# Query-tile norm moved wholly to GpSimd, weight conversion paced by kind of slot, start-up loads interleaved, half steps reordered

## The chip, the cores and the metric

One core of one Trainium2 chip runs the whole program. The metric is device time in microseconds of one execution. TensorE multiplies (PE in the profile, its weight loads PEld), VectorE (DVE) and ScalarE (ACT) work on elements, GpSimd (POOL) does so too, but only on on-chip memory that is not PSUM, and SyncE (SP) issues the transfers. Each engine runs its own instructions strictly in the order in which the program has them, and waits on semaphores for the others.

## The reference

```python
scale = 1.0 / np.sqrt(np.sqrt(D))                 # D = 64, m = 128 features
def phi(x):                                       # q, k: 4 batches, 8 heads, 576 rows
    h = x @ omega.T - np.sum(x * x, -1, keepdims=True) / 2
    return np.exp(h - h.max(-1, keepdims=True)) / np.sqrt(m)
q_p, k_p = phi(q * scale), phi(k * scale)
kv = einsum('bhsm,bhsd->bhmd', k_p, v);  z = k_p.sum(axis=2)
x = (q_p @ kv) / (q_p @ z + 1e-6)                 # to 2304 tokens x 512
xn = x / sqrt(mean(x*x) + 1e-6) * rms_g           # the norm this change moves
g = xn @ w_gate                                   # 512 -> 1536
y = (g * sigmoid(g) * (xn @ w_val)) @ w_out       # 1536 -> 512
h = y @ w_in                                      # 512 -> 2048
out = (h * cos(h)) @ w_out2                       # 2048 -> 512
```

All inputs are float32. The term -sum(x*x)/2 and the 1/sqrt(m) fall out of the quotient, so the kernel does not compute them.

## The kernel before

The 2304 tokens are 18 tiles of 128; a block is 3 tiles (384 columns), so there are 6 blocks. A float32 product is made of three products of float32r halves (`mm3`): every weight chunk of 128 x 512 is split into a high and a low part on the chip ("conversion", class `Weights`).

**Conversion** of one chunk c is a generator: ScalarE writes W (L138), VectorE does four instructions (L153, L155, L157, L160), GpSimd adds (L164), the load of chunk c + 3 is issued on SP, ScalarE rounds to w (L170), GpSimd subtracts (L172). `wts.tick(n)` advances it by n of these seven steps; the instructions land in the engines' queues where the call stands. `wts.pace(rate)` does the same with a fractional count.

**Attention** runs in slots. A slot projects one tile of keys or queries (`project`, 16 matmuls into two PSUM banks), takes the row maxima on VectorE and eight exponentials on ScalarE (`features`). A key tile is multiplied with its values one slot later (`kv_product`). A query tile t goes on through six later steps (`query_step`): 1 turn the features (eT) and copy them out, 2 sums and quotients (num, den, x), 3 square on ScalarE (sq), 4 `root` and `norm`, 5 turn x (xT) and copy the high part (`put(t, 0)`), 6 the low part on VectorE (`put(t, 1)`), after every third tile with a store to DRAM. The norm before is: VectorE scales and shifts the mean square (L281), GpSimd raises it to the power -1/2 (L282), VectorE multiplies x by it and by the gain (L286).

Slots 0 to 22 hold the 18 key tiles and query tiles 0 to 4 (slots 6, 9, 12, 15, 22); from slot 9 to 17 a period is one query tile and two key tiles. From slot 23 on each slot is a half step of the first feed-forward layer: step n is slots 23 + 2n and 24 + 2n, in each the 12 matmuls of `product` (gv) and, for the step before, 6 of `out1` (y), and query tiles 5 to 17 start at slots 24, 26, 29, 32, 34, 37, 40, 42 and so on, three in eight. ScalarE needs another function table for Silu than for the exponential.

PSUM banks with tag "w" (four, handed out in turn) hold gv, qp or kp (two), xT and, in the half steps, also eT and num. A product that gets a bank waits until whoever reads the bank's last holder is done.

Within a slot the order is that of the code: `slot_before` does steps 6 and 4 of older tiles, `slot_after` begins the new tile and does steps 5, 3, 2, 1 of older ones and the key-value product. `manual_schedule` means that the engines get their instructions in this order.

Of the kernel before, what the change touches and what calls it, by code (L numbers as in the profile page):

```python
# [38 lines left out]
AF = mybir.ActivationFunctionType  # L39
ALU = mybir.AluOpType  # L40
# [13 lines left out]
def attention_then_ffn(ctx: ExitStack, tc: tile.TileContext, qT, kT, v, omT, wc1, rms_g, wc2, out, B, H, S, D):  # L54
    nc = tc.nc
    M = omT.shape[1]
    DM = H * D
# [43 lines left out]
    def f32(ap):  # L101
        return ap.bitcast(F32)
# [3 lines left out]
    quarter = const.tile([P, 1], F32, name="quarter")  # L106
    half_pi = const.tile([P, 1], F32, name="half_pi")
# [6 lines left out]
    class Weights:  # L114
# [26 lines left out]
        def run(self):  # L141

            last = len(self.todo)
            for c in range(3):
                self.load(c)
            yield
            self.exponent(0)
            yield
            for c in range(last + 1):
                if c < last:  # L150
                    w, raw = self.w.pop(c), self.raw.pop(c)
                    f = conv.tile([P, 512], I32, tag="f", name=f"f{c}", bufs=3)
                    nc.vector.tensor_scalar(f, w, 3, None, op0=ALU.logical_shift_left)  # L153
                    yield
                    nc.vector.scalar_tensor_tensor(f, w, SIGN, f, op0=ALU.bitwise_and, op1=ALU.bitwise_or)  # L155
                    yield
                    nc.vector.tensor_scalar(raw[:, :, 1], f, SIGN_AND_EXPONENT, None, op0=ALU.bitwise_and)  # L157
                    yield
                    rest = f32(raw[:, :, 1])
                    nc.vector.scalar_tensor_tensor(rest, raw[:, :, 0].bitcast(U32), 2.0 ** -52, rest,  # L160
                                                   op0=ALU.mult, op1=ALU.mult)
                    self.exponent(c + 1)
                    yield
                    nc.gpsimd.tensor_tensor(f32(f), f32(f), rest, op=ALU.add)  # L164
                    self.f[c] = f32(f)
                    yield
                    self.load(c + 3)
                if c > 0:
                    t = wpool.tile([P, 2, 512], F32R, tag="w", name=f"w{c - 1}")
                    nc.scalar.copy(t[:, 0], self.f[c - 1])  # L170
                    yield
                    nc.gpsimd.tensor_tensor(t[:, 1], self.f.pop(c - 1), f32(t[:, 0]), op=ALU.subtract)  # L172
                    self.out[self.todo[c - 1]] = t
                    self.done = c
                    yield
# [20 lines left out]
    wts = Weights()  # L196


    class Attention:
# [41 lines left out]
        def keep_transposed(self, t, r):  # L241
            ps = self.ps.pop(("eT", t, r))
            eT = self.tile_of("featT", [P, HP, P], F32, f"eT{t}_{r}")
            ps = ps.rearrange("p (h n) -> p h n", h=HP)
            if r or self.tag == "w":
                nc.scalar.copy(eT, ps)
            else:
                nc.vector.tensor_copy(eT, ps)
            self.eT[t, r] = eT
# [26 lines left out]
            ms = self.ms[t] = self.tile_of("ms", [P, 1], F32, f"ms{t}")  # L276
            nc.scalar.activation(sq, self.x[t], AF.Square, accum_out=ms)

        def root(self, t):
            ms = self.ms[t]  # L280
            nc.vector.tensor_scalar(ms, ms, 1.0 / DM, 1e-6, op0=ALU.mult, op1=ALU.add)  # L281
            nc.gpsimd.tensor_tensor(ms, ms, minus_half, op=ALU.pow)  # L282

        def norm(self, t):
            a = self.x[t]
            nc.vector.scalar_tensor_tensor(a, a, self.ms.pop(t), self.gain, op0=ALU.mult, op1=ALU.mult)  # L286

        def load_gain(self):
            self.gain = self.tile_of("gain", [P, DM], F32, "gain")
# [32 lines left out]
    with tc.manual_schedule():  # L322
# [7 lines left out]
        att = Attention(  # L330
            lambda what, shape, dt, name: ap.tile(shape, dt, tag=what, name=name, bufs=depth.get(what, 2)), "q", kv)
# [4 lines left out]
        def load_v(t):  # L336
            if t < NTILE:
                nc.sync.dma_start(vt[t % NV][:, 0:H], v[t])
# [28 lines left out]
        def query_step(t, s):  # L367

            if s == 1:
                for r in range(2):  # L370
                    att.transposed(t, r)
                    att.keep_transposed(t, r)
            elif s == 2:
                for r in range(2):
                    att.sums(t, r)
                    att.quotients(t, r)
            elif s == 3:
                att.square(t)
            elif s == 4:
                att.root(t)  # L380
                att.norm(t)
            elif s == 5:
                att.turn(t)
                att.put(t, 0)
            elif s == 6:
                att.put(t, 1)
                if t % TPB == TPB - 1:
                    store(t // TPB, "x")
# [7 lines left out]
        SLOTS = len(tiles)  # L396
# [3 lines left out]
        begins, then = {}, {}  # L400
        for s, (nm, t) in tiles.items():
            if nm == "k":
                for i in range(len(parts(t))):
                    then.setdefault(s + 1 + i, []).append((1, kv_product, t, i))
            else:
                for i in range(1, 7):
                    then.setdefault(s + i, []).append((-i, query_step, t, i))
        for todo in then.values():
            todo.sort(key=lambda e: e[0])
        AHEAD = 2  # L410
        order = sorted(tiles)

        def slot_before(s):

            at = order.index(s) if s in tiles else -1
            if at >= 0 and at + AHEAD < len(order):
                att.load(*tiles[order[at + AHEAD]])
            for k, f, *args in then.get(s, []):
                if k in (-6, -4):
                    f(*args)  # L420

        def slot_after(s):
            if s in tiles:
                att.project(*tiles[s])
                for r in range(2):
                    att.features(*tiles[s], r)
            for k, f, *args in then.get(s, []):
                if k not in (-6, -4):
                    f(*args)

        nc.sync.dma_start(om, omT)
        att.load(*tiles[0])
        att.load(*tiles[1])
        load_v(0)
        wts.tick(1)
        load_v(1)
        load_v(2)
        att.load_gain()
        for a in vt:
            nc.vector.memset(a[:, H], 1.0)  # L440
        for a in kv:
            nc.vector.memset(a[:, H * (D + 1):], 0.0)
        make_identity(nc, ident)
        nc.gpsimd.memset(quarter, 0.25)
        nc.gpsimd.memset(half_pi, math.pi / 2)
        nc.gpsimd.memset(minus_half, -0.5)
        nc.vector.tensor_scalar(om, om, SCALE, None, op0=ALU.mult)

        UP = 9
        for s in range(SLOTS):  # L450
            slot_before(s)
            slot_after(s)
            if wts.done < UP:
                wts.tick(4)


        att.tag = "w"
# [15 lines left out]
        late = [None]  # L473
# [59 lines left out]
        def out1(g, blk, f, t, first, last, es):  # L533

            if first and es[0] == 0:
                yacc[blk] = [bank_of_sums(f"y_ps{g}_{blk}_{f}_{e}")[:, :NB] for e in range(KD)]
            w = wts.get(1, f, 2)
            for e in es:
                mm3(yacc[blk][e], two(w, slice(e * P, (e + 1) * P)), two(t), first, last)
            if not last:  # L540
                return
            for e in es:
                if g == 0:
                    waits.append((put_away, blk, e, yacc[blk][e]))
                else:
                    waits.append((add_up, blk, slice(e * NB, (e + 1) * NB), yacc[blk][e]))
            if g == len(GROUPS1) - 1 and es[-1] == KD - 1:
                for e in range(KD):
                    waits.append((split_y, blk, e))
                waits.append((store, blk, "y"))  # L550
# [77 lines left out]
        steps = steps_of(GROUPS1, orders1)  # L628
# [7 lines left out]
        for n, (g, blk, f, first, last) in enumerate(steps):  # L636
            in_g = len(GROUPS1[g]) * NBLK
            left = in_g - n % in_g - 3
            rate = rate_of(C1 * NF1 // 3 * (g + 2), left) if left > 0 else 0
            if g == 0 and n < G:  # L640
                rate = max(rate, 8)
            if n % in_g == 0:
                wts.freed = C1 * len(GROUPS1[0]) * g
            s = SLOTS + 2 * n
            slot_before(s)
            ps = product(blk, f, 0)
            a = silu(blk, f, ps)
            slot_after(s)
            if n >= 1:
                out1(*steps[n - 1][:3], hid[n - 1], *steps[n - 1][3:], (0, 1))  # L650
            wts.pace(rate / 2)
            flush(3)
            slot_before(s + 1)
            ps = product(blk, f, 1)
            hid[n] = gated(blk, f, a, ps)
            slot_after(s + 1)
            if n >= 1:
                out1(*steps[n - 1][:3], hid.pop(n - 1), *steps[n - 1][3:], (2, 3))
            if n in fetches:
                fetch(fetches[n], f"xhl{g}_{fetches[n]}")  # L660
            if g == 1 and f == GROUPS1[1][1]:
                take_back(blk)
            wts.pace(rate / 2)
            flush(3)
# [83 lines left out]
```

## Time and profile before

| | |
|---|---|
| median of 3 runs | 1034.91 us (1033.3 to 1035.83) |
| the profiled execution: its time, its span | 1034.51 us, 1032.7 us |
| busy: PE, DVE, ACT, POOL | 1001.7, 630.3, 474.8, 191.9 us |
| first gv matmul of the feed-forward part | 102.7 us after the span's start |

The span is what the trace shows from the first to the last instruction; 1.8 us of the execution lie around it. Busy times are unions of instructions on an engine. A matmul's shown duration includes the pipeline's drain, so TensorE's speed is read from the distance between starts, and its idle time from the waits.

### The profile page before, as it was taken

Reading aid. Unit: us, or ns where it says so; the run is one execution under the profiler, and the core shown is the slowest. Engines: PE = TensorE matmul, PEld = TensorE weight load, DVE = VectorE, ACT = ScalarE, POOL = GpSimd, SP = SyncE. Lnnn points to the kernel's source line nnn. Section 1 sums busy time; section 2 is a strip of 40 time slices with the busy share of each in tenths; the row PEclk is TensorE's granted clock in tenths of the full one; section 3 lists DMA queues with packets and bytes.
Section 4 is the critical chain, followed back from the end, with each engine's and each line's share of the span. In section 5 each row is a group of like instructions: output and inputs, shape, how many; then the busy total and the mean of one; then the engine's idle time right before and its main releaser. Section 6 shows DMA issues by size and latency. Waiting matters only on the chain.

```text
span 1032.7 us, 15416 instructions
## 1 busy us (share of the span) xinstructions
PE 1001.7 (97%) x6040; PEld 948.0 (92%) x6040; DVE 630.3 (61%) x1180; ACT 474.8 (46%) x1018; POOL 191.9 (19%) x163
## 2 busy tenths in 40 slices
PE   7979899999999999999999999999999999999998
PEld 6878898998999999999999999878999999999997
DVE  5876575655524555324666337988667777566655
ACT  5766766856722222212333224555545444434443
POOL 1431222221101332102333001333112221000000
PEclk8998999999999999999999999999999999999999
DMA  7545142422221643502455412335202341003401
GB/s 247 205 153 175 63 159 77 163 94 81 112 93 50 246 153 126 190 1 88 160 181 209 158 62 82 123 134 192 82 21 103 121 179 67 2 1 123 153 31 61
DMA packets 32616, 121.90 MB, mean 118 GB/s; under 512 B 3616, under 2 KB 9888, under 8 KB 27936
## 3 DMA queue, kind: packets, MB, share of 16 engines
q1 hardware_dynamic: 32544, 120.93, 32.7%
q8 instruction: 47, 0.77, 0.3%
q14 instruction: 25, 0.20, 0.1%
HBM read 92.60 MB, written 28.31 MB: 117 GB/s over the span
## 4 chain that ended last, share of the span: by engine, by line
PE 72%; DVE 3%; ACT 1%; issue 0%; POOL 0%
PE gv_ps L462 8%; PE gv_ps L461 8%; PE gv_ps L463 8%; PE o_ps L463 6%; PE h_ps L463 6%; PE h_ps L461 6%; PE h_ps L462 6%; PE o_ps L462 6%; PE o_ps L461 6%; PE y_ps L461 4%; PE y_ps L462 4%; PE y_ps L463 4%; PE num_ps L258 1%; DVE o L574 1%; DVE turns L564 0%
## 5 line engine op out<-in xcount | busy, mean ns | idle before, releaser
L461 PE MATMUL gv_ps<-xhl,w 128*128 128x384 f32 x576 | 192.8, 335 | 1.8 <-DVE den L268 1.8
L463 PE MATMUL gv_ps<-xhl,w 128*128 128x384 f32 x576 | 192.6, 334 | 0.0
L462 PE MATMUL gv_ps<-xhl,w 128*128 128x384 f32 x576 | 192.4, 334 | 0.0
L164 POOL TENSOR_TENSOR f<-f,raw 128x512 f32<-128x512 f32 x68 | 90.2, 1326 | 530.9 <-issue 304.2
L463 PE MATMUL h_ps<-yhl,w 128*128 128x384 f32 x384 | 129.5, 337 | 0.0
L461 PE MATMUL h_ps<-yhl,w 128*128 128x384 f32 x384 | 129.3, 337 | 0.0
L462 PE MATMUL h_ps<-yhl,w 128*128 128x384 f32 x384 | 129.0, 336 | 0.0
L526 DVE TENSOR_TENSOR gv<-gv_ps,gv 128x384 f32<-128x384 f32 x72 | 40.1, 557 | 141.6 <-PE gv_ps L463 134.7
L527 ACT CAST t<-gv 128x384 fp32r<-128x384 f32 x72 | 37.0, 513 | 193.6 <-DVE gv L526 193.6
L463 PE MATMUL o_ps<-w,o 128*128 128x512 f32 x288 | 114.4, 397 | 0.6 <-DVE o L574 0.4
L462 PE MATMUL o_ps<-w,o 128*128 128x512 f32 x288 | 113.7, 395 | 0.0
L461 PE MATMUL o_ps<-w,o 128*128 128x512 f32 x288 | 112.4, 390 | 1.0 <-DVE osum L584 0.6
L569 ACT ACTIVATE turns<-turns,half_pi 128x384 f32<-128x384 f32 x96 | 59.3, 617 | 114.6 <-DVE turns L564 114.6
L461 PEld LDWEIGHTS gv_ps<-xhl,w 128*128 128x128 f32 x576 | 108.1, 188 | 2.4 <-issue 1.2
L462 PEld LDWEIGHTS gv_ps<-xhl,w 128*128 128x128 f32 x576 | 108.1, 188 | 0.0
L463 PEld LDWEIGHTS gv_ps<-xhl,w 128*128 128x128 f32 x576 | 108.1, 188 | 0.0
L172 POOL TENSOR_TENSOR w<-f,w 128x512 fp32r<-128x512 f32 x68 | 92.2, 1356 | 79.0 <-ACT w L170 49.2
L461 PE MATMUL y_ps<-t,w 128*128 128x384 f32 x288 | 99.5, 345 | 0.0
L463 PE MATMUL y_ps<-t,w 128*128 128x384 f32 x288 | 96.4, 335 | 0.0
L462 PE MATMUL y_ps<-t,w 128*128 128x384 f32 x288 | 96.4, 335 | 0.0
L574 DVE TENSOR_TENSOR o<-turns,o 128x384 fp32r<-128x384 f32 x96 | 61.4, 639 | 47.0 <-ACT o L572 47.0
L572 ACT CAST o<-turns 128x384 fp32r<-128x384 f32 x96 | 49.3, 514 | 75.5 <-DVE turns L571 74.5
(72 smaller groups left out, 1771.7 us busy)
## 6 DMA issues: line engine op xcount, KB each, us to landing
raw<-wc SPq DMA_DIRECT2D x68, 512.0 KB, 3.6
yhl<-y_dram SPq DMA_DIRECT2D x14, 1536.0 KB, 6.9
xhl<-x_dram SPq DMA_DIRECT2D x10, 1536.0 KB, 8.2
x_dram<-xhl SPq DMA_DIRECT2D x6, 1536.0 KB, 5.1
y_dram<-yhl SPq DMA_DIRECT2D x6, 1536.0 KB, 7.3
kraw<-kT SPq DMA_DIRECT2D x18, 256.0 KB, 3.8
v<-v SPq DMA_DIRECT2D x18, 256.0 KB, 3.0
qraw<-qT SPq DMA_DIRECT2D x18, 256.0 KB, 3.7
```

What stands on the lines that cost most here:

```text
L164: nc.gpsimd.tensor_tensor(f32(f), f32(f), rest, op=ALU.add)
L172: nc.gpsimd.tensor_tensor(t[:, 1], self.f.pop(c - 1), f32(t[:, 0]), op=ALU.subtract)
L258: nc.tensor.matmul(ps[p0:p0 + n, h * P:(h + 1) * P], eT[:, h, p0:p0 + n], self.kv[b][:, at:at + P], start=True, stop=True, skip_group_chec ...
L461: nc.tensor.matmul(o, w[0], x[0], start=first, stop=False)
L462: nc.tensor.matmul(o, w[0], x[1], start=False, stop=False)
L463: nc.tensor.matmul(o, w[1], x[0], start=False, stop=last)
L526: nc.vector.tensor_tensor(a, ps, a, op=ALU.mult)
L527: nc.scalar.copy(t[:, 0], a)
L569: nc.scalar.activation(r, r, AF.Sin, bias=half_pi)
L572: nc.scalar.copy(o[:, 0], r)
L574: nc.vector.tensor_tensor(o[:, 1], r, f32(o[:, 0]), op=ALU.subtract)
```

## The change

The norm becomes four GpSimd instructions (scale and shift, power, x times the root, times the gain), and VectorE has none of it. Conversion is no longer advanced by 4 steps per slot until 9 chunks are done, but by 5 in slots 1 to 5, 2 in slots 6 to 17 and 4 in slots 18 to 22. The first three weight loads, the value loads and the gain's load are spread over slots 0 to 3, and an exponential at the very start loads ScalarE's table. In slots 0 to 22 the order of steps is 6, begin, 5, 4, 3, 2, 1, key-value product. In the half steps it is product, Silu, steps 5, 4, 3, 2, 6, begin, out1, step 1; step 6 comes one slot earlier there, in the slot of step 5. The copy of the first half of eT is on VectorE in the half steps too.

```diff
-            for c in range(3):
-                self.load(c)
-            yield
             self.exponent(0)
...
-            if r or self.tag == "w":
+            if r:
                 nc.scalar.copy(eT, ps)
...
-        def root(self, t):
-            ms = self.ms[t]
-            nc.vector.tensor_scalar(ms, ms, 1.0 / DM, 1e-6, op0=ALU.mult, op1=ALU.add)
+        def norm(self, t):
+            a, ms = self.x[t], self.ms.pop(t)
+            nc.gpsimd.tensor_scalar(ms, ms, 1.0 / DM, 1e-6, op0=ALU.mult, op1=ALU.add)
             nc.gpsimd.tensor_tensor(ms, ms, minus_half, op=ALU.pow)
-
-        def norm(self, t):
-            a = self.x[t]
-            nc.vector.scalar_tensor_tensor(a, a, self.ms.pop(t), self.gain, op0=ALU.mult, op1=ALU.mult)
+            nc.gpsimd.tensor_scalar(a, a, ms, None, op0=ALU.mult)
+            nc.gpsimd.tensor_tensor(a, a, self.gain, op=ALU.mult)
...
-                    then.setdefault(s + i, []).append((-i, query_step, t, i))
+                    late = s + i - (s + i > SLOTS and i == 6)
+                    then.setdefault(late, []).append((-i, query_step, t, i))
...
-        wts.tick(1)
-        load_v(1)
-        load_v(2)
-        att.load_gain()
+        nc.gpsimd.memset(quarter, 0.25)
+        nc.scalar.activation(half_pi, quarter, AF.Exp)
...
-        UP = 9
         for s in range(SLOTS):
-            slot_before(s)
-            slot_after(s)
-            if wts.done < UP:
-                wts.tick(4)
+            load_ahead(s)
+            if s < 3:
+                if s:
+                    load_v(s)
+                wts.load(s)
+            if s == 3:
+                att.load_gain()
+            older(s, -6)
+            begin(s)
+            older(s, -5, -4, -3, -2, -1, 1)
+            if s:
+                wts.tick(5 if s < 6 else 2 if s < 18 else 4)
...
-            slot_before(s)
+            load_ahead(s)
             ps = product(blk, f, 0)
             a = silu(blk, f, ps)
-            slot_after(s)
+            older(s, -5, -4, -3, -2, -6)
+            begin(s)
             if n >= 1:
                 out1(*steps[n - 1][:3], hid[n - 1], *steps[n - 1][3:], (0, 1))
+            older(s, -1, 1)
```

The second half step is changed in the same way. Three places in the engines' orders follow.

SP at the program's start, before (kraw are tiles of keys, v of values, raw weight chunks of 512 KB, om the projection):

```order
L431 DMA om_73<-omT 128x128
L210 DMA kraw0_93<-kT 128x512
L210 DMA kraw1_95<-kT 128x512
L338 DMA v0_89<-v 128x512
L132 DMA raw0_98<-wc1 128x1024
L132 DMA raw1_100<-wc1 128x1024
L132 DMA raw2_102<-wc1 128x1024
L338 DMA v1_90<-v 128x512
L338 DMA v2_91<-v 128x512
L290 DMA gain_106<-rms_g 128x512
L210 DMA kraw2_123<-kT 128x512
```

SP at the same place in the change:

```order
L425 DMA om_73<-omT 128x128
L207 DMA kraw0_93<-kT 128x512
L207 DMA kraw1_95<-kT 128x512
L333 DMA v0_89<-v 128x512
L207 DMA kraw2_114<-kT 128x512
L132 DMA raw0_116<-wc1 128x1024
L207 DMA kraw3_142<-kT 128x512
L333 DMA v1_90<-v 128x512
L132 DMA raw1_145<-wc1 128x1024
L333 DMA v0_89<-v 128x512
L207 DMA kraw4_191<-kT 128x512
```

The third key tile's load stood behind three weight chunks, two value tiles and the gain; now it stands ahead of all of them.

GpSimd in slots 29 and 30 (step 3), before; f is a conversion's add, w its subtraction, ms6 the norm of query tile 6:

```order
L164 TENSOR_TENSOR f13_1524<-f13_1524,raw13_1266 128x512
L172 TENSOR_TENSOR w12_1580<-f12_1396,w12_1580 128x512
L282 TENSOR_TENSOR ms6_1630<-ms6_1630,minus_half_76 128x1
L164 TENSOR_TENSOR f14_1639<-f14_1639,raw14_1391 128x512
L172 TENSOR_TENSOR w13_1692<-f13_1524,w13_1692 128x512
```

GpSimd there in the change:

```order
L161 TENSOR_TENSOR f13_1577<-f13_1577,raw13_1341 128x512
L169 TENSOR_TENSOR w12_1646<-f12_1473,w12_1646 128x512
L278 TENSOR_SCALAR ms6_1605<-ms6_1605 128x1
L279 TENSOR_TENSOR ms6_1605<-ms6_1605,minus_half_76 128x1
L280 TENSOR_SCALAR x6_1556<-x6_1556,ms6_1605 128x512
L281 TENSOR_TENSOR x6_1556<-x6_1556,gain_241 128x512
L161 TENSOR_TENSOR f14_1690<-f14_1690,raw14_1468 128x512
```

The norm is four instructions in a row, behind the subtraction of chunk 12, which waits for ScalarE's w12.

TensorE in slot 34 (the second half of step 5), where query tile 9 begins, 8 is summed and 7 is turned; before:

```order
L463 MATMUL gv_ps1_1_1_1868<-xhl1_1152,w4_579 128x384
L220 MATMUL qp_ps9_0_1885<-om_73,qraw9_1582 128x128
L220 MATMUL qp_ps9_1_1886<-om_73,qraw9_1582 128x128
...
L296 MATMUL xT_ps7_1909<-ident_72,x7_1722 128x128 x4
L258 MATMUL num_ps8_0_1915<-kv1_86,eT8_0_1841 128x128 x4
L258 MATMUL num_ps8_1_1925<-kv1_86,eT8_1_1848 128x128 x4
L461 MATMUL y_ps0_1_0_2_1852<-t1_0_1769,w2_421 128x384
```

TensorE there in the change:

```order
L461 MATMUL gv_ps1_1_1_1871<-xhl1_1130,w4_772 128x384
L291 MATMUL xT_ps7_1888<-ident_72,x7_1724 128x128 x4
L255 MATMUL num_ps8_0_1894<-kv1_86,eT8_0_1856 128x128 x4
L255 MATMUL num_ps8_1_1904<-kv1_86,eT8_1_1863 128x128 x4
L217 MATMUL qp_ps9_0_1914<-om_73,qraw9_1581 128x128
L217 MATMUL qp_ps9_1_1915<-om_73,qraw9_1581 128x128
...
L459 MATMUL y_ps0_1_0_2_1843<-t1_0_1773,w2_422 128x384
```

The projection went from ahead of the older tiles' products to behind them.

## Rows read from the trace of the kernel before

**Rows 1.** Windows: us, busy us (instructions) by engine, granted clock, DMA share, GB/s.

```profile
0.00:28.30 28.30, 21.32 (x179) 20.03 (x181) 15.09 (x33) 16.07 (x51) 6.53 (x14) 0.88 0.69 235
28.30:85.90 57.60, 47.83 (x448) 44.12 (x445) 45.46 (x95) 40.05 (x129) 20.59 (x18) 0.91 0.50 170
...
102.70:286.00 183.30, 174.43 (x1278) 166.97 (x1277) 108.80 (x243) 127.11 (x273) 40.55 (x39) 1.00 0.30 106
```

**Rows 2.** Waits of PE in 0:28.3, 28.3:102.7, 102.7:300: total us, times, longest.

```profile
PE kp_ps L220 <- DMA kraw<-kT: 7.0, 2, 3.8
...
PE xT_ps L296 <- ACT ke L231: 7.9, 3, 3.7
...
PE num_ps L258 <- DVE x L270: 5.1, 3, 2.2
PE gv_ps L461 <- DVE den L268: 1.8, 2, 0.9
PE num_ps L258 <- DVE gv L526: 1.2, 1, 1.2
```

**Rows 3.** Timeline of the first 30 us: start, us, engine and instruction, idle before.

```profile
7.56 2.85 PE L350 MATMUL kv_ps<-v,ke 128*128 128x128 f32 x16
...
9.42 0.43 DVE L153 TENSOR_SCALAR f<-W 128x512 int32<-128x512 int32 x1 [2.20 <-ACT W L138]
...
13.54 2.08 PE L220 MATMUL kp_ps<-om,kraw 64*128 64x128 f32 x16 [3.14 <-DMA kraw<-kT]
...
28.07 0.37 PE L220 MATMUL qp_ps<-om,qraw 64*128 64x128 f32 x1
```

**Rows 4.** Timeline of ACT and DVE around the third query tile's norm.

```profile
71.48 2.18 ACT L231 ACTIVATE qe<-qp_ps,qmx 128x128 f32<-128x128 f32 x8 [2.86 <-DVE qmx L229]
73.50 0.68 ACT L277 ACTIVATE sq<-x 128x512 f32<-128x512 f32 x1
...
76.66 0.75 DVE L286 SCALAR_TENSOR_TENSOR x<-x,ms,gain 128x512 f32<-128x512 f32 x1 [2.21 <-POOL ms L282]
77.33 1.28 DVE L229 TENSOR_REDUCE kmx<-kp_ps 128x4 f32<-128x512 f32 x2
```

**Rows 5.** Timeline of PE over the periods of query tiles 1 to 3.

```profile
40.48 1.16 PE L220 MATMUL qp_ps<-om,qraw 64*128 64x128 f32 x16
...
53.14 1.16 PE L220 MATMUL qp_ps<-om,qraw 64*128 64x128 f32 x16
54.23 2.05 PE L350 MATMUL kv_ps<-v,ke 128*128 128x128 f32 x16
...
63.52 0.82 PE L296 MATMUL xT_ps<-ident,x 128*128 128x128 f32 x4 [2.42 <-ACT ke L231]
...
69.30 1.16 PE L220 MATMUL qp_ps<-om,qraw 64*128 64x128 f32 x16
...
79.31 1.12 PE L296 MATMUL xT_ps<-ident,x 128*128 128x128 f32 x4 [3.65 <-ACT ke L231]
```

**Rows 6.** Chain that ended last, pieces with nothing in their way: start, us.

```profile
267.33 0.44 PE xT_ps L296 x4
267.77 1.79 PE num_ps L258 x16
```

**Rows 7.** Groups by form in 0:260: count, busy us, mean ns, idle before.

```profile
L164 POOL TENSOR_TENSOR f<-f,raw 128x512 f32<-128x512 f32 x22 | 28.6, 1302 | 107.4 <-issue 87.4 <-DVE raw L160 20.0
...
L231 ACT ACT_TABLE_LOAD x13 | 16.7, 1283 | 2.2 <-DVE qmx L229 1.3 <-PEq L740 0.7
...
L155 DVE SCALAR_TENSOR_TENSOR f<-W,f 128x512 int32<-128x512 int32 x22 | 16.2, 736 | 0.6
...
L282 POOL TENSOR_TENSOR ms<-ms,minus_half 128x1 f32<-128x1 f32 x15 | 8.2, 549 | 37.3 <-DVE ms L281 37.2
```

**Rows 8.** Timeline of step 2, a GpSimd add and a VectorE instruction beside it.

```profile
127.34 1.36 POOL L164 TENSOR_TENSOR f<-f,raw 128x512 f32<-128x512 f32 x1 [7.00 <-issue]
...
127.58 1.68 DVE L155 SCALAR_TENSOR_TENSOR f<-W,f 128x512 int32<-128x512 int32 x1
```

More of the change, by code (lines that the diff above doesn't have):

```diff
@@ L379, in query_step @@
             elif s == 4:
-                att.root(t)
                 att.norm(t)
@@ L411, in attention_then_ffn, with load_ahead @@
         order = sorted(tiles)
-        def slot_before(s):
+        def load_ahead(s):
             at = order.index(s) if s in tiles else -1
@@ L417, in slot_before, with older, begin @@
                 att.load(*tiles[order[at + AHEAD]])
[L418 to L422, printed above, removed]
+        def older(s, *steps):
+            for step in steps:
+                for k, f, *args in then.get(s, []):
+                    if k == step:
+                        f(*args)
+        def begin(s):
             if s in tiles:
@@ L426, in slot_after @@
                     att.features(*tiles[s], r)
-            for k, f, *args in then.get(s, []):
-                if k not in (-6, -4):
-                    f(*args)
         nc.sync.dma_start(om, omT)
@@ L443, in attention_then_ffn @@
         make_identity(nc, ident)
-        nc.gpsimd.memset(quarter, 0.25)
         nc.gpsimd.memset(half_pi, math.pi / 2)
@@ L644, in attention_then_ffn @@
             s = SLOTS + 2 * n
-            slot_before(s)
+            load_ahead(s)
             ps = product(blk, f, 0)
             a = silu(blk, f, ps)
-            slot_after(s)
+            older(s, -5, -4, -3, -2, -6)
+            begin(s)
             if n >= 1:
                 out1(*steps[n - 1][:3], hid[n - 1], *steps[n - 1][3:], (0, 1))
+            older(s, -1, 1)
             wts.pace(rate / 2)
             flush(3)
-            slot_before(s + 1)
+            load_ahead(s + 1)
             ps = product(blk, f, 1)
             hid[n] = gated(blk, f, a, ps)
-            slot_after(s + 1)
+            older(s + 1, -5, -4, -3, -2, -6)
+            begin(s + 1)
             if n >= 1:
                 out1(*steps[n - 1][:3], hid.pop(n - 1), *steps[n - 1][3:], (2, 3))
+            older(s + 1, -1, 1)
             if n in fetches:
```

## Prediction

> **What bounds the kernel now.** I read the windows first, cut where the program changes character [rows 1]: the first 28.3 us (key tiles 0 to 5), 28.3 to 85.9 (the periods of one query and two key tiles), and 102.7 to 286 (half steps with query tiles). The change touches nothing behind these; there TensorE stands still for little. In the first stretch TensorE is busy 21.3 of 28.3 us, in the second 47.8 of 57.6, in the third 174.4 of 183.3. No engine is full in the second: VectorE has 45.5 of 57.6, ScalarE 40.1, GpSimd 20.6. So what can be won there is latency between engines. TensorE's waits by stretch [rows 2] say where: 7.0 us for key tiles at the start, of which 3.8 is the first landing that nothing can hide; 7.9 us ahead of three xT turns; and in the half steps 5.1 + 1.8 + 1.2 = 8.1 us ahead of num and gv. Each such wait loses about 0.2 us more than it shows, since the pipeline's drain counts as busy; 8.1 in seven waits is about 9.5.
>
> **Start (gain 4.0, from 0 to 6).** The third projection begins at 13.54, after 3.14 us of waiting for its load [rows 3], which stands on SP behind three weight chunks of 512 KB, two value tiles and the gain. In the change it stands fifth. TensorE is free when the key-value product of tile 0 ends at 7.56 + 2.85 = 10.4, so 3.1 us go. VectorE's f of chunk 0 waited for ScalarE's W until 9.42 with tile 1's maxima behind it; now those come first. But chunk 0's four VectorE instructions (about 2.2 us) then stand ahead of tile 2's maxima, and their W stands on ScalarE behind tile 1's exponentials, near 11. Tile 2's maxima start near 13.9 where its projection ends near 11.4, so 2.5 us come back. From there to query tile 0 I count tiles 2 to 5 at about 3.3 us, each bound by maxima, two to four conversion instructions and exponentials: its projection starts near 24.1 to 24.3, where it was 28.07. If the loads do no better than before, the gain is 0; without the 2.5 us it would be 6.
>
> **Periods of query tiles 1 to 3 (gain 9.4, from 4 to 13).** The row to see is the x of the third norm [rows 4]: VectorE sits 2.21 us until GpSimd's power is done, then needs 0.75, and only then come the maxima of the next key tile at 77.33, though their projection had long ended. Their exponentials free the PSUM bank for xT, so xT starts at 79.31 after 3.65 us of TensorE's idling; for the tile before 2.42 [rows 5]. These periods last 16.2 us (53.14 to 69.30) and 16.6 (69.30 to the stretch's end at 85.9), the first 12.7 (40.48 to 53.14): 45.4 together. In the two long ones the granted clock also halves after the idling: 0.91 of the stretch [rows 1] is 9% of 57.6 us missing, twice that, 10 us, at half speed.
>
> Now the norm leaves VectorE and conversion there takes 2 steps per slot instead of 4. What ends xT's wait is then GpSimd. From the start of a query tile's projection: 1.1 for it (1.16 with its drain [rows 5]), 0.9 until the first exponential, 2.0 for eight, and the square ends 2.7 after the first exponential [rows 4] plus about 0.3 for its accumulator: 5.0. GpSimd then has four instructions in a row. The power takes 0.55, the product with the gain 1.30 as every 128x512 product of two tensors there [rows 7]. The trace has no one-input GpSimd instruction of this size: it is bounded above by that 1.30 and below by 0.43, VectorE's for one (the f in [rows 3]); I take 0.8. The 128x1 scale lies between almost nothing and the power's 0.55; I take 0.2. Together 2.85, from 2.3 to 3.7. xT can start at 7.8; then 0.44 and 1.79 for the sums [rows 6], 1.9 for the key-value product (2.05 with its drain [rows 5]): a period of 12.0. Three are 36, against 45.4: gain 9.4. It is 4 if one clock drop and half the blocking remain, 13 if xT never waits. The Trainium skill's page "GPSIMD Engine Reference", section 4.1, calls one-input work there about line rate and two-input work about half VectorE's speed; its first half would make the scaling some 0.5 (an estimate from that page) and the gain about 1 us more. No row here has the one-input form.
>
> **Slots 18 to 22 (loss 1.0, from 0 to 2.5).** Before, conversion had stopped there (9 chunks done) and TensorE is busy throughout; now it takes 4 steps a slot, and the norm of tile 3 stands on GpSimd behind an add whose VectorE work comes late. I price it at one late turn.
>
> **Half steps: order (loss 0.3, from -5 to +3).** The waits of 9.5 us go, since the projection no longer takes banks ahead of num. Three times in this stretch (slots 34, 42, 50) a tile is turned, one summed and one begun in one slot. There qp's second bank is xT's, which is free after step 6 on VectorE, behind both quotients. VectorE comes to them about 2.2 us after gv ends (product, ScalarE's cast, subtraction: three of 0.5 to 0.6), needs 0.8 each and 0.7 for step 6; TensorE has only 0.44 + 1.79 to fill: a wait of about 2.1, three times 6.4. Once (slot 28) gv must wait 2.1 for a bank whose Silu stands behind a table load of 1.28 [rows 7] and the exponentials of a projection that is now later. Two waits of together 1.3 for eT of tile 5 and num make 9.8.
>
> **Half steps: GpSimd (loss 7.8, from 0 to 13).** This is the new wait. From the square of tile t to its turn lie almost two slots, some 8 us, enough for 2.85. But GpSimd is in order, and in four cases (tiles 6, 9, 10, 11) the norm stands right behind a conversion's subtraction that waits for ScalarE's w, which the program has behind the exponentials of the tile begun in that slot. For tile 6, from slot 29's start: projection ends 3.6, maxima end at 5.3 behind step 6, table load and exponentials until 8.0, W and w until 9.4, subtraction 10.7, norm 13.6; TensorE reaches xT at 10.8. So 2.8 for tile 6, and in the same way 2.0, 2.4 and 0.6. In the others the instruction ahead is done early. The bounds are no wait at all, if ScalarE is 3 us earlier than I count, and 1.3 more on each.
>
> **Shared work.** Where a VectorE instruction of two on-chip inputs meets one of GpSimd it stretches: 1.68 us beside an add [rows 8], against 0.736 on average [rows 7]. The Trainium skill's page "SBUF — State Buffer", section "Who interferes with whom", states this as an exclusive lock: the later of the two is held for the whole of the other's instruction. By it each of the two long GpSimd instructions of a norm can hold a conversion step for up to its length. On this trace such a step is mostly off the path, so the sum has nothing for it; its price is in the slow case below. VectorE sheds 0.9 per tile with the norm and gains a copy of 0.7 in the half steps, ScalarE sheds that copy: no term. The early table load replaces one that already ran before the first exponential: no gain.
>
> **Sum.** -4.0 - 9.4 + 1.0 + 0.3 + 7.8 = -4.3 on the profiled execution's 1034.51, which is 0.4 below the median of the runs: 1030.2. I say 1030, with its own range 1025 to 1035.
>
> **Rivals.** (1) GpSimd keeps up in the half steps: 7.8 falls away and the norm is at its short end; 1030.2 - 7.8 - 1.5 = 1021. For it: GpSimd has 40.6 us of work in 183 [rows 1], and 13 norms add some 30 to the powers already in it; ScalarE has 56 us to spare. Against it: the order, which makes it wait for ScalarE. (2) The change moves the wait and no more: in the periods xT waits for GpSimd as long as it did for VectorE, the start gives its 4 and the half steps take that back: 1034 to 1036. For it: the undisturbed first period was 12.7 with the norm on VectorE, and I get 12.0. Against it: 16.2 and 16.6. (3) Slower: a norm of 4.2 us, from a slow one-input form or from being held by VectorE. Then xT waits 1.35 longer in three periods and for the four late turns, 9.5 in all, and one more turn becomes late: 1040. It decides from a norm of 3.5 us on (4.3 over seven turns is 0.6 each); against it speaks that all four instructions at their upper bounds make 3.7.
>
> **How the numbers follow.** Two results within 0.3% (3.1 us) cannot be told apart here. Forecast 0.45 (0.30 of it faster by more, 0.13 same, 0.02 slower), rival 1 0.25 (faster), rival 2 0.15 (0.01 faster, 0.13 same, 0.01 slower), rival 3 0.15 (slower, 0.01 of it same). That is 0.56 faster, 0.27 same, 0.17 slower. The range 1018 to 1040 takes in rival 1 with a good start and rival 3.
>
> **What would show it.** kp of the third tile starting near 10.4 and query tile 0 near 24; xT's waits in the periods 1 to 2 us, put down to GpSimd; no clock drop between 28 and 80; the first gv near 90; in the half steps xT waits for GpSimd at tiles 6, 9 and 10, and qp waits for VectorE three times. The forecast is wrong if a one-input GpSimd product takes over 1.5 us, if the first gv comes after 97, or if xT never waits behind slot 23.

## The result

The changed kernel takes **1043.33 us** (median of 8 runs, 1038.32 to 1046.44) where the kernel before takes 1035.42 in the runs beside it (8 runs, 1032.32 to 1037.14): a ratio of 1.0072, 95% interval 1.0048 to 1.0096. It is slower, by more than the 0.3% that can be told from nothing, and above the range. The profiled execution took 1044.52 us with a span of 1042.7.

The windows of the changed kernel, cut at its own marks (query tile 0 starts at 25.4, the slots of the last key tiles at 83.6, the first gv at 104.6, the end of the half steps with query tiles at 308.3), and then the stretches in which the granted clock was at its lower level:

```profile
0.00:25.40 25.40, 19.30 (x176) 17.96 (x176) 16.76 (x35) 16.42 (x53) 6.75 (x14) 1.00 0.78 261
25.40:83.60 58.20, 49.88 (x446) 46.35 (x446) 35.22 (x74) 36.17 (x122) 21.35 (x21) 0.88 0.44 141
83.60:104.60 21.00, 18.50 (x182) 17.48 (x181) 15.48 (x25) 13.03 (x43) 9.31 (x8) 0.92 0.64 226
104.60:308.30 203.70, 189.89 (x1342) 181.70 (x1342) 117.06 (x239) 126.07 (x268) 91.24 (x84) 0.98 0.30 101
47.50:51.00 3.50, 3.50 (x19) 3.50 (x18) 1.28 (x6) 0.76 (x3) 0.32 (x1) 0.51 0.00 0
61.20:68.00 6.80, 5.93 (x28) 5.93 (x29) 2.03 (x8) 3.03 (x10) 2.05 (x2) 0.50 0.03 11
78.30:81.70 3.40, 3.40 (x19) 3.40 (x18) 0.76 (x3) 1.65 (x6) 1.90 (x2) 0.50 0.45 141
95.30:98.80 3.50, 3.50 (x19) 3.27 (x19) 1.85 (x2) 1.67 (x3) 2.87 (x3) 0.51 0.10 39
150.00:156.80 6.80, 6.11 (x26) 6.11 (x27) 2.12 (x7) 1.58 (x3) 3.15 (x3) 0.50 0.28 80
```

Set against [rows 1]: the start is shorter (25.4 us for 28.1) and at full clock. The periods take as long as before, though VectorE has 35.2 us of work there in place of 45.5: the work was taken away and the time stayed. GpSimd's work in the half steps is 91.2 us, against 41.1 over the same instructions of the kernel before (102.7 to 297.0 there). What TensorE waits for there, beside [rows 2] (first line 25.4 to 104.5, the others 104.5 to 300):

```profile
PE xT_ps L291 <- POOL x L281: 10.5, 4, 3.2
...
PE xT_ps L291 <- POOL x L281: 12.5, 7, 3.6
PE gv_ps L459 <- DVE den L265: 0.8, 1, 0.8
```

One kind of wait that matters is left, eleven times and 23.0 us in all (the others come to 2.6): the turn of a query tile waits for the last instruction of its norm, on GpSimd. The waits for num of [rows 2] are gone from the half steps. The periods on TensorE, beside [rows 5]:

```profile
37.86 1.16 PE L217 MATMUL qp_ps<-om,qraw 64*128 64x128 f32 x16
...
46.65 0.65 PE L291 MATMUL xT_ps<-ident,x 128*128 128x128 f32 x4 [2.44 <-POOL x L281]
47.14 3.24 PE L255 MATMUL num_ps<-kv,eT 128*128 128x128 f32 x16
50.17 2.33 PE L345 MATMUL kv_ps<-v,ke 128*128 128x128 f32 x16
52.44 1.16 PE L217 MATMUL qp_ps<-om,qraw 64*128 64x128 f32 x16
...
62.07 1.11 PE L291 MATMUL xT_ps<-ident,x 128*128 128x128 f32 x4 [3.16 <-POOL x L281]
62.98 3.62 PE L255 MATMUL num_ps<-kv,eT 128*128 128x128 f32 x16
66.39 2.74 PE L345 MATMUL kv_ps<-v,ke 128*128 128x128 f32 x16
69.06 1.16 PE L217 MATMUL qp_ps<-om,qraw 64*128 64x128 f32 x16
...
77.78 0.68 PE L291 MATMUL xT_ps<-ident,x 128*128 128x128 f32 x4 [2.37 <-POOL x L281]
...
83.56 1.16 PE L217 MATMUL kp_ps<-om,kraw 64*128 64x128 f32 x16
```

From 37.86 (query tile 1) the periods last 14.6, 16.6 and 14.5 us: 45.7, where 36 were forecast and 45.4 stood before. The sums behind the turn take 3.0 to 3.4 us from start to start (47.14 to 50.17, 62.98 to 66.39) in place of 1.79 [rows 6]: they run wholly or mostly at half clock. And the norm itself, first undisturbed beside query tile 1, then for tile 6 in the half steps, then by form over 0:260:

```profile
42.73 0.19 POOL L278 TENSOR_SCALAR ms<-ms 128x1 f32<-128x1 f32 x1 [3.14 <-ACT sq L274]
43.01 0.57 POOL L279 TENSOR_TENSOR ms<-ms,minus_half 128x1 f32<-128x1 f32 x1
43.67 1.57 POOL L280 TENSOR_SCALAR x<-x,ms 128x512 f32<-128x512 f32 x1
45.33 1.27 POOL L281 TENSOR_TENSOR x<-x,gain 128x512 f32<-128x512 f32 x1
...
144.50 1.28 POOL L169 TENSOR_TENSOR w<-f,w 128x512 fp32r<-128x512 f32 x1 [1.36 <-ACT w L167]
145.87 0.38 POOL L278 TENSOR_SCALAR ms<-ms 128x1 f32<-128x1 f32 x1
...
147.27 2.03 POOL L280 TENSOR_SCALAR x<-x,ms 128x512 f32<-128x512 f32 x1
149.38 1.26 POOL L281 TENSOR_TENSOR x<-x,gain 128x512 f32<-128x512 f32 x1
```

```profile
L280 POOL TENSOR_SCALAR x<-x,ms 128x512 f32<-128x512 f32 x14 | 23.2, 1657 | 1.4
L281 POOL TENSOR_TENSOR x<-x,gain 128x512 f32<-128x512 f32 x14 | 18.4, 1311 | 1.2
L279 POOL TENSOR_TENSOR ms<-ms,minus_half 128x1 f32<-128x1 f32 x14 | 9.7, 692 | 1.2
```

The product with one tensor and one value per partition takes 1.57 us where nothing disturbs it, longer than the product of two tensors (1.27); the distances between starts on GpSimd say the same (1.66 from 43.67 to 45.33, 1.22 from there to the next instruction at 46.55). The norm is 3.87 us from its first start to its last end, not 2.85. For tile 6 the row ahead of it is the conversion's subtraction, which came 1.36 us late because it waited for ScalarE's w. That is exactly the row that the prediction named; the turn follows at 150.69.

### The profile page after: what moved, and what is told of

It is laid out like the page before. It is cut to its first block, busy times and chain, and to the rows that moved or that the text cites. A ratio compares the mean times of both kernels' runs of the same rounds, so it can differ in the third digit from the quotient of the medians.

```text
span 1042.7 us, 15446 instructions
## 1 busy us (share of the span) xinstructions
PE 1007.7 (97%) x6040; PEld 953.4 (91%) x6040; DVE 629.3 (60%) x1158; ACT 469.5 (45%) x1005; POOL 251.0 (24%) x217
## 4 chain that ended last, share of the span: by engine, by line
PE 78%; DVE 8%; ACT 6%; POOL 5%; issue 2%; DMA 1%; SPq 0%; POOLq 0%; DVEq 0%; ACTq 0%
PE gv_ps L461 8%; PE gv_ps L459 8%; PE gv_ps L460 8%; PE h_ps L461 5%; PE h_ps L459 5%; PE h_ps L460 5%; PE o_ps L460 5%; PE o_ps L461 5%; PE o_ps L459 5%; PE y_ps L459 4%; PE y_ps L461 4%; PE y_ps L460 4%; PE num_ps L255 3%; PE kv_ps L345 2%; POOL x L280 2%; ACT qe L228 2%
## 5 line engine op out<-in xcount | busy, mean ns | idle before, releaser
L572 DVE TENSOR_TENSOR o<-turns,o 128x384 fp32r<-128x384 f32 x96 | 58.7, 612 | 43.8 <-ACT o L570 43.8
```

Source lines behind the costliest of these rows:

```text
L572: nc.vector.tensor_tensor(o[:, 1], r, f32(o[:, 0]), op=ALU.subtract)
```

## The experiments

Three marks in each profiled execution say where time is won or lost: the start of query tile 0, the first gv, and from there to the first h (which holds all half steps with query tiles). Times in us; each ratio is against runs of the kernel before on the same chip.

| kernel | median (runs) | ratio to before, 95% | query 0 | first gv | gv to h |
|---|---|---|---|---|---|
| before | 1035.42 (8) | | 28.07 | 102.72 | 518.9 |
| changed | 1043.33 (8) | 1.0048 to 1.0096 | 25.44 | 104.58 | 528.2 |
| e1 changed, old norm | 1025.01 (5) | 0.9885 to 0.9918 | 24.98 | 92.57 | 520.7 |
| e2 before, norm moved | 1041.90 (6) | 1.0049 to 1.0086 | 27.26 | 105.06 | 522.6 |
| e3 before, half-step order | 1034.95 (12) | 0.9982 to 1.0005 | 27.36 | 104.54 | 518.2 |
| e4 before, slots 0 to 22 | 1022.55 (5) | 0.9861 to 0.9895 | 25.05 | 93.12 | 518.0 |
| e5 changed, norm early | 1022.93 (6) | 0.9853 to 0.9896 | 23.96 | 94.32 | 512.1 |
| e6 changed, norm short | 1017.11 (5) | 0.9806 to 0.9836 | 25.86 | 90.10 | 515.6 |
| e7 changed, filled | 1036.56 (12) | 1.0004 to 1.0039 | 23.92 | 96.69 | 528.4 |
| e8 changed, spread product | 1035.43 (12) | 0.9990 to 1.0012 | 25.01 | 99.08 | 526.2 |
| e9 early and spread | 1018.81 (4) | 0.9832 to 0.9866 | 24.69 | 92.98 | 512.9 |
| e10 early, on VectorE | 1045.62 (4) | 1.0087 to 1.0118 | 24.12 | 105.24 | 529.2 |
| e11 before, norm moved early | 1036.36 (11) | 0.9986 to 1.0021 | 26.34 | 99.36 | 520.8 |
| e12 e9, filled | 1017.45 (4) | 0.9822 to 0.9849 | 24.09 | 92.88 | 512.4 |

e3 changes nothing ahead of the first gv and yet has it 1.8 us later than before: single executions differ by about 2 us in that column, so only larger differences there are read as findings. The profiled execution is one of the runs: that of e5 is 4.8 us below its median and that of e11 3.4, the others lie within 1.6.

**Taking the change apart (e1 to e4).** e1 and e2 differ from the changed kernel and from the one before by this alone:

```
-            nc.vector.tensor_scalar(ms, ms, 1.0 / DM, 1e-6, op0=ALU.mult, op1=ALU.add)
+            nc.gpsimd.tensor_scalar(ms, ms, 1.0 / DM, 1e-6, op0=ALU.mult, op1=ALU.add)
             nc.gpsimd.tensor_tensor(ms, ms, minus_half, op=ALU.pow)
-            nc.vector.scalar_tensor_tensor(a, a, ms, self.gain, op0=ALU.mult, op1=ALU.mult)
+            nc.gpsimd.tensor_scalar(a, a, ms, None, op0=ALU.mult)
+            nc.gpsimd.tensor_tensor(a, a, self.gain, op=ALU.mult)
```

(e1 has the lines with a minus, e2 those with a plus.) e3 is the kernel before with the loop over the half steps, the earlier sixth step and the eT copy of the change:

```
-            slot_before(s)
+            load_ahead(s)
             ps = product(blk, f, 0)
             a = silu(blk, f, ps)
-            slot_after(s)
+            older(s, -5, -4, -3, -2, -6)
+            begin(s)
...
+            older(s, -1, 1)
```

e4 is the kernel before with the start and the loop over slots 0 to 22 of the change (one load of a weight chunk in each of the first three slots, the table's load at the head, conversion in 5, 2 and 4 steps).

> All of the change but the norm, which is done as before (VectorE's scaling of ms, GpSimd's power, VectorE's one pass over x). Theory A, the norm on GpSimd costs the time: its 3.87 us from the first instruction to the last stand ahead of the turn, and behind a conversion's subtraction in the half steps; the changed kernel's turns waited 13.9 us there and 2.7 more in the slots behind the queries. Without it the first gv comes about 4 us earlier and the half steps about 9 shorter: 1030 us, 1026 to 1033. Theory B, the norm is hidden and the new order of the half steps, the pacing and the loads cost the time: 1040 to 1046, as the changed kernel.

> The kernel before with nothing changed but the norm: its four instructions on GpSimd, at the norm's place. Theory A: slower, since GpSimd still has four conversions in every slot of the queries and the norm queues behind their subtractions; turns wait 1 to 3 us longer in the queries and in the half steps: 1044 us, 1039 to 1050. Theory B: 1034, as before, since the work taken off VectorE pays for the longer chain.

> The kernel before with only the new order of the half steps (older tiles first, put's second half a slot earlier after the last slot, first copy of eT on VectorE); norm as before. Theory A: 1030 us, 1026 to 1034: the 9.5 us of waits that the half steps of before have in their old order mostly go, as they did in the changed kernel, and no wait of a turn takes their place; all of the time from the first gv on is gained or lost here, the slots before it are unchanged. Theory B: 1040 or more, the half steps take the 9.3 us more that they take in the changed kernel.

> The kernel before with only the change up to the first gv, norm as before: loads and table spread, conversions paced 5, 2, 4 by kind of slot, the order within a slot. Theory A: first gv at 97 to 99 us (102.7 before): 2.6 us from the start, and 1 to 3 from GpSimd and ScalarE having fewer conversions beside the queries; 1030 us, 1027 to 1033. Theory B: the first gv comes at 104 to 105 as in the changed kernel, 1036 or more.

The sign is Theory A's in three cases of four: without the moved norm the change is 1% faster, the moved norm alone makes the kernel before 0.7% slower, and the slots alone win. In e3 it is neither theory's: the order of the half steps is worth nothing in time, where 5 us were expected. The slots alone won 12.5 us in the medians and e1 won 10, where 5 were expected of each. Which part of the slots won it (the pace of the conversion, the order inside a slot, the loads) was not taken apart. The turns beside the queries in e1, on TensorE:

```profile
45.63 0.63 PE L290 MATMUL xT_ps<-ident,x 128*128 128x128 f32 x4 [1.89 <-DVE x L280]
...
58.91 0.63 PE L290 MATMUL xT_ps<-ident,x 128*128 128x128 f32 x4 [0.89 <-DVE x L280]
...
71.44 0.63 PE L290 MATMUL xT_ps<-ident,x 128*128 128x128 f32 x4 [1.90 <-DVE x L280]
```

No turn waits for ScalarE's exponentials as in [rows 5], and none waits 2 us. From the changed kernel to e1 the first gv comes 12.0 us earlier and the half steps are 7.5 shorter: the moved norm's price in this kernel, against 7 us in e2. The same four instructions cost less in e2. There the turns beside the queries wait 9.3 us for GpSimd, where the kernel before waited 7.9 for the exponentials anyway [rows 2]; that the norm runs beside this older wait fits these numbers, but no run shows it by itself.

**What in the norm costs (e5 to e8).** The four kernels are the changed one with one edit each: e5 issues the norm with the square (step 3, where the change has step 4), e6 leaves out one product, e7 gives TensorE something to do in the wait, e8 writes the one-input product as one of two inputs.

```
e5:             elif s == 3:
                    att.square(t)
-               elif s == 4:
                    att.norm(t)
e6: -           nc.gpsimd.tensor_scalar(a, a, ms, None, op0=ALU.mult)
e7: +           if t < 4:
    +               for i in range(8):
    +                   nc.tensor.transpose(ps[:, (i % KD) * P:(i % KD + 1) * P], ident, ident)
e8: -           nc.gpsimd.tensor_scalar(a, a, ms, None, op0=ALU.mult)
    +           nc.gpsimd.tensor_tensor(a, a, ms.to_broadcast([P, DM]), op=ALU.mult)
```

> The changed kernel with the norm's four instructions issued right behind the square, one step earlier, so that on GpSimd they stand ahead of the conversions of the step between. Theory A1, a good part of the norm's price is the queue ahead of it on GpSimd (a conversion's subtraction that waits for ScalarE): the turns' waits of 13.9 us in the half steps fall to 5 or less, the periods of the queries stay at 14 to 16 us: 1034 us, 1031 to 1038. Theory A2, its price is only the length of its own chain of 3.87 us: the same waits, 1041 to 1046.

> The changed kernel without the product of x by ms on GpSimd (this leaves out a part of the computation: x is only multiplied by the gain), so the chain is 1.57 us shorter, 2.3 us. Theory A2, the length of the chain decides: each period 2 to 2.5 us shorter and no turn's wait long enough for the half clock, first gv at 95 to 98 us; each wait in the half steps 1.0 to 1.5 shorter, half of them gone: 1029 us, 1025 to 1033. Rival: what counts is that GpSimd does the norm at all, in its queue and with VectorE beside it, not how long; the periods stay at 14 us and more: 1037 to 1043.

> The changed kernel with eight transposes of the identity into the turn's own bank ahead of the turns of query tiles 0 to 3, where TensorE waits 2.6 to 3.4 us; they need nothing and take about 1.3 us, less than the wait. Theory C, half of what the norm costs beside the queries is the half clock after those waits (rows of the changed kernel: 17 us at half clock in the first 103): the clock stays full there and the first gv comes at 97 to 100: 1037 us, 1034 to 1040. Rival: TensorE isn't what sets the periods, so its clock costs nothing there: first gv at 104 to 106, 1042 to 1046.

> The changed kernel with the product of x by ms as a tensor_tensor product whose second input is ms spread along the row, in place of the tensor_scalar form. If GpSimd's price hangs on the form and not on the bytes read, it takes 1.28 us as the product by the gain does, not 1.57, and each chain is 0.3 shorter: 1041 us, 1038 to 1044. If an operand that is one value per partition is what costs, it stays at 1.5 or more and the time at 1041 to 1046.

**e5** is 20 us faster than the changed kernel, more than theory A1 gave it. In its half steps no turn waits at all: gv to h is 16 us shorter than in the changed kernel and 6.8 shorter than before. On GpSimd, tile 6's norm (145.87 in the timeline above) now stands ahead of the conversions of the step between and follows its square at once:

```profile
128.28 0.28 POOL L278 TENSOR_SCALAR ms<-ms 128x1 f32<-128x1 f32 x1 [0.77 <-ACT sq L274]
...
130.98 1.30 POOL L281 TENSOR_TENSOR x<-x,gain 128x512 f32<-128x512 f32 x1
132.24 1.30 POOL L161 TENSOR_TENSOR f<-f,raw 128x512 f32<-128x512 f32 x1
```

Beside the queries the place in the order changes little: the norm takes 3.87 us there in both, and the first three turns wait 2.44, 2.31 and 2.38 us (2.44, 3.16 and 2.37 in the changed kernel). Only the fourth, in the slots of the last key tiles, falls from 2.50 to 0.41:

```profile
45.67 0.66 PE L291 MATMUL xT_ps<-ident,x 128*128 128x128 f32 x4 [2.44 <-POOL x L281]
...
59.90 0.66 PE L291 MATMUL xT_ps<-ident,x 128*128 128x128 f32 x4 [2.31 <-POOL x L281]
```

Yet the first gv came 10.3 us earlier: 1.5 of it from the start, 3 from these waits, and the rest, some 6, goes with the clock, which never fell in this execution (mean 1.000). Its other runs have 0.993 to 0.997 and are 3 to 8 us longer. That part of the gain is the clock's, and it isn't steady.

**e7** prices the clock. With the eight transposes in the wait, the turns beside the queries still wait for GpSimd (timeline of TensorE):

```profile
46.43 0.66 PE L294 MATMUL xT_ps<-ident,x 128*128 128x128 f32 x4 [1.31 <-POOL x L281]
...
60.23 0.66 PE L294 MATMUL xT_ps<-ident,x 128*128 128x128 f32 x4 [1.27 <-POOL x L281]
```

and yet the granted clock is full (windows, 40 to 96 us), where the changed kernel had 0.88 and 0.92:

```profile
40.00:96.00 56.00, 49.84 (x505) 45.57 (x505) 38.73 (x75) 38.34 (x128) 26.37 (x25) 1.00 0.54 178
```

The first gv comes at 96.69, 7.9 us earlier (1.5 of it from the start), the half steps are unchanged, and the median falls by 6.8. Theory C holds, the rival (TensorE's clock costs nothing there) falls. The runs say so too: ten of the twelve have mean clocks of 0.993 to 0.997, and the two with 0.990 take 1042.99 and 1044.53, as the changed kernel does.

**e6**, with a norm of 2.07 us, is the fastest of these four, and 12 us below what was expected: the length counts. (It leaves out a part of the computation, so it prices the length and no more.) Its periods are 11.1, 12.0 and 11.1 us, 3.4 to 4.6 shorter than the changed kernel's, and its clock never falls there. **e8** keeps all of the work and its product by ms takes 1.04 us where nothing disturbs it; the groups by form in 0:260:

```profile
L281 POOL TENSOR_TENSOR x<-x,gain 128x512 f32<-128x512 f32 x15 | 20.8, 1384 | 1.2
L280 POOL TENSOR_TENSOR x<-x,ms 128x512 f32<-128x512 f32 x15 | 16.1, 1076 | 1.2
```

1.08 us on average for 1.66: the form sets the price. Some 0.5 us less in each chain (3.35 for 3.87 where nothing disturbs it) took 7.9 us off the median, where 2 were expected from 0.3; the first gv comes 5.5 earlier. The turns' waits fall from 23.0 us to 17.2 in all. Beside the queries they are 1.93, 2.58, 1.79 and 1.92, and the clock falls after three of them for about 3.5 us each (after all but the longest), where it fell after all four in the changed kernel. So a term of 0.5 per tile is worth more than its own sum.

**Putting it together (e9 to e12).** e9 has the edits of e5 and e8; e12 adds that of e7 to e9. e10 is e1 with the norm issued at step 3, as in e5, but on VectorE; e11 is e2 with the norm at step 3.

> The changed kernel with both mends: the norm issued right behind the square, and x times ms as a tensor_tensor product with ms spread along the row. Theory A (place in the queue and length of the chain, each through TensorE's waits): no wait of a turn in the half steps, waits beside the queries under 2 us as with the spread product alone, and so no half clock: first gv at 92 to 95 us, 1018 us, 1015 to 1021. Rival: with the place mended the length no longer counts: 1021 to 1025, as the early norm alone.

> The changed kernel with the norm as before (VectorE, GpSimd for the power alone) but issued right behind the square. If the place in the order is all, it is as good as the early norm on GpSimd or better: 1021 us, 1018 to 1024. If VectorE, which takes its instructions in order, stands still for ScalarE's square and then for the power, and the copies of eT and the quotients behind it come late, it is slower than with the norm a step later: 1027 us, 1024 to 1032.

> The kernel before with nothing changed but the norm: its four instructions on GpSimd, right behind the square. Theory A: the queue on GpSimd was most of the 6.8 us that the norm cost at its old place; the half steps come out as before or up to 5 us shorter, the slots of the queries 0 to 2 longer: 1033 us, 1029 to 1037. Rival: there the chain's length alone costs: 1039 to 1044.

> As the kernel with both mends, with eight transposes of the identity ahead of the turns of query tiles 0 to 3, which need nothing and take 1.3 us. If what is left of TensorE's waits there (under 2 us) still costs clock in some executions, this is 2 to 4 us faster than without them and spreads less; if not, it is the same or up to 2 us slower, where the eight take longer than the wait.

**e9** came as forecast: 1018.81, 16 us faster than before, with three waits for GpSimd left, all beside the queries. Of these 16 the slots alone give 12.5 (e4). The comparison that prices the norm alone is e1: 6 us slower, with intervals that don't meet. TensorE's waits of 0 to 300 us in e9 have this line:

```profile
PE xT_ps L291 <- POOL x L281: 5.4, 3, 1.9
```

**e12** has less than half of it, and 1017.45; four runs each don't tell the two apart.

```profile
PE xT_ps L294 <- POOL x L281: 2.2, 3, 0.8
```

**e10** is as slow as the changed kernel, 14 us beyond the slower of the two cases expected: the same early place that is worth 20 us on GpSimd costs 20 on VectorE. VectorE stands still until the square is done and again for the power, with the next maxima behind it (timeline of VectorE):

```profile
58.73 0.15 DVE L278 TENSOR_SCALAR ms<-ms 128x1 f32<-128x1 f32 x1 [2.26 <-ACT sq L274]
59.55 0.75 DVE L280 SCALAR_TENSOR_TENSOR x<-x,ms,gain 128x512 f32<-128x512 f32 x1 [0.67 <-POOL ms L279]
```

The turns then wait for the exponentials that these maxima feed, three times beside the queries, and the sums wait for the copy of eT, which stands behind the norm on VectorE in the half steps; in TensorE's waits of 0 to 300 us:

```profile
PE xT_ps L290 <- ACT ke L228: 9.1, 3, 3.2
PE num_ps L255 <- DVE eT L245: 8.7, 7, 2.3
```

**e11** lies at the upper end of its range: the early place gives back 5.5 of the 6.8 us that the moved norm cost in the kernel before, and so ends where that kernel was, not 2 below. The place of the gain is not the expected one: the half steps are 2 us longer than before and not shorter, and the old order's waits of num for x, 5.7 us in three, are still there. In the kernel before, the norm on GpSimd is no gain. With the slots of the change it is 2 us ahead of e1 by the same early place (e5; the intervals overlap) and 6 with the spread product (e9).

## Why the prediction was wrong

The step that failed is "The trace has no one-input GpSimd instruction of this size: it is bounded above by that 1.30 and below by 0.43 [...]; I take 0.8". It takes 1.57 us. The upper bound came from a row of another form and holds only if fewer inputs never take longer; the rows of the changed kernel show the contrary, and e8 shows the two-input form of the same product at 1.04. With it the norm is 3.87 us, past the 3.5 from which rival 3 was said to decide, and rival 3 is what came, 3 us longer than its 1040. Both signs named for a wrong forecast (over 1.5 us, first gv after 97) were there. The second fault is in that rival's price and in the term of the periods: a late turn was priced by its wait alone, 1.35 us each. The half clock behind it was seen in [rows 1] but got no term in the sum or in rival 3; only the low end of the periods' range has one drop in it. e7 prices it at 6.8 us. By its terms:

- **Start, 4.0.** Right in kind, too large in size. The third projection started at 10.77 (10.4 forecast); query tile 0 at 25.44, 2.6 us earlier than before. Over all executions it starts at 23.9 to 25.9 in the ten kernels with the new start and at 26.3 to 28.1 in the four with the old one, 24.7 and 27.3 on average: about 2.5 won. That tile 2's maxima stand behind chunk 0's four instructions is there too:

```profile
11.63 0.43 DVE L150 TENSOR_SCALAR f<-W 128x512 int32<-128x512 int32 x1 [2.57 <-ACT W L138]
...
13.89 1.28 DVE L226 TENSOR_REDUCE kmx<-kp_ps 128x4 f32<-128x512 f32 x2
```

- **Periods, 9.4.** Lost whole: 45.7 for 36. Its way of counting held: e6's chain, 0.78 shorter than the 2.85 assumed, should give 11.2 by the same sum, and its periods are 11.1, 12.0, 11.1. With the true chain it gives 13.0, and e7, at full clock, has 13.0, 13.8, 12.9: 39.6 together. So about 3.6 of the missing 9.7 is the longer chain and about 6 the half clock behind the waits that it makes. What the prediction did not see is that most of this gain never hung on the move. In e1, with the norm on VectorE, the same three periods last 38.3 us (37.40 to 75.71), 7.1 less than before, and in e2, where the norm alone is moved, 48.3 (39.67 to 88.00). The row that it built on, VectorE's 2.21 us of waiting for the power [rows 4], was an exception: for that tile a conversion's subtraction stood ahead of the power on GpSimd. For the two tiles before it VectorE waited 0.67, as it does in e1 (timelines of GpSimd before and of VectorE in e1):

```profile
74.85 1.27 POOL L172 TENSOR_TENSOR w<-f,w 128x512 fp32r<-128x512 f32 x1 [3.19 <-DMA v<-v]
76.08 0.55 POOL L282 TENSOR_TENSOR ms<-ms,minus_half 128x1 f32<-128x1 f32 x1
...
58.01 0.75 DVE L280 SCALAR_TENSOR_TENSOR x<-x,ms,gain 128x512 f32<-128x512 f32 x1 [0.67 <-POOL ms L279]
```

- **Slots 18 to 22, 1.0.** 21.0 us for 16.9: 4.1 lost. e1 has 16.9 there with the same conversions, so they cost nothing and the loss is one late turn of tile 3, its wait of 2.50 us and 3.5 us at half clock behind it.
- **Order of the half steps, 0.3.** Right in the sum (e3: -0.7 from gv to h, no change in time), wrong inside: the old waits were counted as seven where [rows 2] has six, 0.2 us too much; the three waits of qp for xT's bank, 6.4, did not come (1.2 in two waits of qp in e3), and smaller ones ahead of gv and xT stand beside them. e1 is 2.5 us above e4, whose half steps have the old order; their intervals overlap, and whether the order costs something there stays open.
- **GpSimd in the half steps, 7.8.** The mechanism was right, and e5 shows it: with the norm ahead of the conversions every one of these waits is gone. The tiles were right as well: tiles 6, 9, 10 and 11 wait 3.61, 3.05, 3.19 and 0.66 us where 2.8, 2.0, 2.4 and 0.6 were forecast, the first three 0.8 to 1.1 more, about what the norm is longer (1.0). Three short waits of other tiles (1.10, 0.42, 0.48) make it 12.5 in seven. The half clock from 150.0 to 156.8 comes on top; behind the waits of 3.05 and 3.19 the clock did not fall.
- **Shared work, no term.** It had one on the path: beside VectorE's instructions the norms of tiles 6 and 9 take 4.77 us each (145.87 to 150.64, 190.85 to 195.62) in place of 3.87.

The Trainium skill's page "GPSIMD Engine Reference", section 4.1, was cited with one-input work at about line rate. For this form the trace disagrees: 1.57 us for 512 elements per partition.

## What to carry to other kernels

An operation without a row in the trace has no upper bound from a row of another form; where the forecast hangs on it, the other form of the same arithmetic is worth a try (here 0.5 us per product, and 8 us of time). An instruction that waits belongs on an engine that has nothing urgent behind it, and there as early as it can stand: the same early norm won 20 us on GpSimd and lost 20 on VectorE. A stall of TensorE may be paid twice, once as the wait and once as half clock behind it (here behind waits of 1.8 to 3.6 us, but not behind every one), so read the granted clock behind each wait before pricing it; idle TensorE can be given harmless work. And a gain that a forecast puts down to two edits at once is worth a run with each alone: here the pace and the order of the slots had most of it (12.5 us), and the moved norm, as first written, took it back.

## What was not expected of the hardware

- GpSimd's product of 128x512 by one value per partition takes 1.57 us; by a second tensor 1.27; by the same value spread along the row as a second input 1.04 (e8, undisturbed).
- The clock did not fall by the length of the wait alone: after a wait of 2.44 us it fell in the changed kernel (0.51 from 47.5), after one of 2.44 at the same place in e5 it did not, and in e1 it was 0.66 in 46 to 51 after 1.89. Within the changed kernel it fell after 2.37 (77.78) and not after 3.05 and 3.19 (195.68 and 212.89). The runs of one kernel spread with it: the changed kernel's have mean clocks of 0.987 to 0.994 and times from 1046.44 to 1038.32. The Trainium skill's page "TensorE: Matmul & The Clock Gate", Part 1, says that the point at which the clock rises to full differs from run to run. What differs here is whether it falls at all; the page's point on the rise is not shown by any run here. What decides in a single case was not found.
